# Four PSUM banks for the second product behind attention, and router constants made later

## The chip, the cores and the metric

The program runs on one core of one Trainium2 chip. The metric is the time of one execution on the device in microseconds (us). The kernel before has a median of 832.97 us over three runs (830.79, 832.97 and 835.6).

## The reference

Attention (512 local and 32 global keys, 4 batches, 8 heads) gives x of 2176 tokens by 512. A feed-forward layer follows, and then eight experts, to which a router gives the tokens.

```
def _moe_ref(x, w_in, w_out, alpha):
    h = x @ w_in                                        # 2176 x 512 by 512 x 2048
    g = np.maximum(h, 0.0) + alpha * np.minimum(h, 0.0)
    return (g @ w_out).astype(np.float32)               # 2176 x 2048 by 2048 x 512

def _moe2_ref(x, w_gate, w1, w2):
    logits = x @ w_gate
    order = np.argsort(-logits.flatten())
    # in this order each token goes to its best expert that has room (2176 // 8 = 272 tokens)
    for e in range(E):
        mask = assigned == e
        h = np.maximum(x[mask] @ w1[e], 0.0)
        out[mask] = h @ w2[e]
```

## The kernel before

The tokens are cut into eight blocks (c = 0 to 7) of 272. The hidden width of 2048 is cut into two halves (hf = 0, 1) of eight tiles of 128 (f = 0 to 7). Products are in three terms: each operand is split into a high half (a copy on ACT, L72) and a low half (a subtraction, L73, on DVE or on POOL), and TensorE adds high by high, low by high and high by low.

All eight blocks first pass through half 0 in `gemm`. The first product (`gemm1`, L196) makes tile f in 12 matmuls into a PSUM bank; ACT makes `neg` (L201), DVE makes `g` (L202), ACT its high half `ghi` and POOL its low half `glo`. The second product (L230) makes four outputs d = 0 to 3, each of 8 tiles by three terms, 24 matmuls: 96 for a block. ACT copies each output out of its bank into `xd` (L236; two buffers), and SP sends it to `xpart` in DRAM (L237). The second product has one pool of two banks, `pY`: outputs 2 and 3 reuse the banks of 0 and 1. The order is: output 0 and output 1 over tiles 0 to 5, output 0 and output 1 over tiles 6 and 7, then output 2 and output 3 over all eight tiles.

While attention runs (blocks 0 to 2 and a part of block 3), attention and `gemm` take turns. Behind attention a pool `pO` of two banks is opened, and the first product takes its banks from `pH` (two banks) and `pO` in turn, which is what the list `odd` says (it is empty under attention). In this stretch the weights of half 1 are decoded beside the products (lines 83 to 92; every seventh step, so many steps being six matmuls each), and TensorE turns decoded parts of `w_out` (L132, L140, L146) between the steps. Then half 1's first product runs for all blocks in `gemm1b`, with the logits; then half 1's second product with the router beside it; then the experts.

The order of TensorE's instructions is the order of the program, written out by hand. ACT, DVE, POOL and SP work through queues whose order a planner makes beforehand from a simulated timeline: what is ready goes first, and of what is ready, what stands first in the program. Each engine works its queue in order. `tc.issue_after(x)` puts an edge from each instruction traced in its block to x, but only for the instructions on the engine of x.

Behind the last block of half 0 stand the router's constants (L691 to L779): index tables made by iotas on POOL, small conversions on DVE, and eight memsets on POOL (`ohs`, `gs`, `vas`, `sbs`, twice each). After them stands `splitx(0, 1)`, which makes the high and low halves of block 0 for half 1: `xh` on ACT, `xl` on DVE.

Of the kernel before, what the change touches and what calls it, by code (L numbers as in the profile page):

```python
# [9 lines left out]
F32 = mybir.dt.float32  # L10
# [15 lines left out]
def tile_attention_moe_moe(ctx: ExitStack, tc: tile.TileContext, qkw, vw,  # L26
# [10 lines left out]
    KD = DM // 128  # L37
# [5 lines left out]
    KH = KF // 2  # L43
    CH = CAP
    NCH = NTOK // CH
    CPB = ST // CH
# [24 lines left out]
    def split(hi, lo, src, lo_eng=None):  # L71
        a = A.copy(hi, src)  # L72
        return a, (lo_eng or V).tensor_tensor(lo, src, hi.bitcast(F32), op=OP.subtract)  # L73
# [84 lines left out]
    pH = ctx.enter_context(tc.tile_pool(name="pH", bufs=2, space=PSUM))  # L158
    g1 = ExitStack()
    pY = g1.enter_context(tc.tile_pool(name="pY", bufs=2, space=PSUM))  # L160

    X, XB, alt = {}, {}, {}

    def loadx(c, hf):
        cs = slice(c * CH, (c + 1) * CH)
        X[c, hf] = [None, None]
        if hf:
            t = gx.tile([128, 2, KD, CH], F32, name="xb", bufs=2)
            for i, src in enumerate((xs, xpart)):
                nc.sync.dma_start(out=t[:, i], in_=src[:, :, cs].rearrange("k p t -> p k t"))  # L170
                X[c, hf][i] = t[:, i]

    def splitx(c, hf):
        if hf and c in alt:
            xh, xl = alt[c]
        else:
            xh = gx.tile([128, KD, CH], F32R, name="xh")
            xl = gx.tile([128, KD, CH], F32R, name="xl")
        split(xh, xl, X[c, hf][0] if hf else XB[c // CPB][:, :, (c % CPB) * CH:(c % CPB + 1) * CH])
        X[c, hf] += [xh, xl]  # L180

    post = []
    epi = [None]
    ybank = [pY, "y"]
    odd = []

    def gemm1(c, hf, f, g):
        _, _, xh, xl = X[c, hf]
        wi = WI[hf]
        pool, tag = odd[0] if odd and f % 2 else (pH, "h1")  # L190
        ps = pool.tile([128, CH], F32, name="h1", tag=tag)
        fs = slice(f * 128, (f + 1) * 128)
        i = 0
        for k in range(KD):
            for w, x in ((0, xh), (0, xl), (1, xh)):
                T.matmul(ps, wi[:, w, k, fs], x[:, k], start=i == 0, stop=i == 3 * KD - 1)  # L196
                i += 1
            if k % 2 == 1 and k < KD - 1:
                yield 0.7
        neg = gh_.tile([128, CH], F32, name="neg")  # L200
        A.activation(out=neg, in_=ps, func=AF.Relu, scale=-1.0)  # L201
        epi[0] = V.scalar_tensor_tensor(g, neg, al1[:, hf * KH + f:hf * KH + f + 1], ps, op0=OP.mult, op1=OP.add)  # L202

    def gemm(c, hf, nxt):
        if len(X[c, hf]) < 3:
            splitx(c, hf)
        if nxt is not None:
            loadx(*nxt)
        gh = gt_.tile([128, KH, CH], F32R, name="ghi", tag="ghi")
        gl = gt_.tile([128, KH, CH], F32R, name="glo", tag="glo")  # L210
        wo = WO[hf]
        for f in range(KH):
            g = gh_.tile([128, CH], F32, name="g")
            yield from gemm1(c, hf, f, g)
            split(gh[:, f], gl[:, f], g, lo_eng=P)
            if post:
                post.pop(0)()
            yield 0.7
        if (c + 1, hf) in X:
            splitx(c + 1, hf)  # L220
        ys = {}
        for d, fs in [(0, range(KH - 2)), (1, range(KH - 2)), (0, range(KH - 2, KH)), (1, range(KH - 2, KH))] + [
                (d, range(KH)) for d in range(2, KD)]:
            if d not in ys:
                ys[d] = ybank[0].tile([128, CH], F32, name="y", tag=ybank[1])
            ps = ys[d]
            ds_ = slice(d * 128, (d + 1) * 128)
            for f in fs:
                for i, (w, x) in enumerate(((0, gh), (0, gl), (1, gh))):
                    T.matmul(ps, wo[:, w, f, ds_], x[:, f], start=f == 0 and i == 0, stop=f == KH - 1 and i == 2)  # L230
                if f % 2 == 1 and f < KH - 1:
                    yield 0.7
            if fs[-1] < KH - 1:
                continue
            xd = gx.tile([128, CH], F32, name="xd", bufs=2)
            A.copy(xd, ps)  # L236
            nc.sync.dma_start(out=xpart[d, :, c * CH:(c + 1) * CH], in_=xd)  # L237
            yield 0.7
        X[c, hf] = None
# [25 lines left out]
    LR = 512  # L265
# [22 lines left out]
    def gemm1b(c, nxt):  # L288
        pt = X[c, 1][1]
        for f in range(KH):  # L290
            yield from gemm1(c, 1, f, gbt(c, f))
            if post and f % 2:
                post.pop(0)()
            if f == 0 and nxt is not None:
                loadx(*nxt)
            if f == 4 and nxt is not None:
                splitx(*nxt)
            yield 0.7
        lp = []
        post.append(lambda: lp.append(logits(c, pt)))  # L300
        post.append(lambda: lput(c, lp[0]))

    with ExitStack() as at:
# [308 lines left out]
        c = 0  # L612
        g = None
        going = True
        while going:
            want = c if g is None else c + 1
            if want < NCH and (want, 0) not in X and done[0] >= (want // CPB + 1) * UPB - 1 and (
                    g is None or len(X[c, 0]) == 4):
                loadx(want, 0)
            if g is None and (c, 0) in X:  # L620
                g = gemm(c, 0, None)
            if spent["a"] <= spent["g"] * ratio or g is None:
                x = next(att, None)
                if x is None:
                    going = False
                else:
                    spent["a"] += x
            else:
                x = next(g, None)
                if x is None:  # L630
                    g = None
                    c += 1
                else:
                    spent["g"] += x
                    if parts:
                        f, i = parts.pop(0)
                        with tc.issue_after(at_norm[UPB // 2 - 1, STEPS - 1].ins):
                            f(dc, 0, i)
                    else:
                        share[0] = False  # L640
# [4 lines left out]
    with tc.tile_pool(name="dc2", bufs=1, side="right") as dc, tc.tile_pool(name="pW", bufs=2, space=PSUM) as pW, \  # L645
            tc.tile_pool(name="pO", bufs=2, space=PSUM) as pO:
        odd.append((pO, "h3"))
        more = []
        parts = [(win_part, i) for i in range(2 * KD)] + [(wout_part, i) for i in range(KH)]
        n = 0  # L650
        while c < NCH:
            if g is None:
                if (c, 0) not in X:
                    loadx(c, 0)
                g = gemm(c, 0, (c + 1, 0) if c + 1 < NCH else None)
            while next(g, None) is not None:
                n += 1
                if n % 7 == 0 and parts:
                    f, i = parts.pop(0)
                    with tc.issue_after(epi[0].ins):  # L660
                        more += [(n + 11 + 3 * j, x) for j, x in enumerate(f(dc, 1, i) or [])]
                if more and n >= more[0][0]:
                    more.pop(0)[1]()
            g = None
            c += 1
        assert not parts
        for _, f in more:
            f()
    NDEF = 8
    DEF = list(range(NCH - NDEF, NCH))  # L670
    with ExitStack() as mo:
        rc_ = mo.enter_context(tc.tile_pool(name="rc_", bufs=1, side="right"))
        g2 = ExitStack()
        gx2 = g2.enter_context(tc.tile_pool(name="gx2", bufs=1, side="right"))
        g1.close()
        p4 = mo.enter_context(tc.tile_pool(name="q4", bufs=2, space=PSUM))
# [1 line left out]
        px = mo.enter_context(tc.tile_pool(name="qx", bufs=1, space=PSUM))  # L678
        ph = mo.enter_context(tc.tile_pool(name="qh", bufs=1, space=PSUM))
        pm = mo.enter_context(tc.tile_pool(name="qm", bufs=2, space=PSUM))  # L680
        ybank[:] = [p4, "h4"]

        SH = [26, 20, 15, 10, 5, 0]
        TH = [64, 64, 32, 32, 32, 32]
# [2 lines left out]
        MAGIC = 0x4B000000  # L687
        MF = float(1 << 23)
        MR = 1.5 * MF
        ip = rc_.tile([128, 1], I32, name="ip")  # L690
        P.iota(ip, [[0, 1]], base=0, channel_multiplier=1)  # L691
        ipf = rc_.tile([128, 1], F32, name="ipf")
# [78 lines left out]
        for i in range(2):  # L771
# [5 lines left out]
            P.memset(vas[i], 0.0)  # L777
            sbs.append(rc_.tile([128, NP, 32], BF, name=f"sbs{i}"))
            P.memset(sbs[i], 0.0)  # L779
        Lrow = gx2.tile([128, LR], F32, name="Lrow")  # L780
        loadx(0, 1)
        splitx(0, 1)
        GT = 30
        gbs = [wa.tile([128, GT, CH], F32, name="gb", tag=t) for t in ("wa1", "wa0")]
        gbs.append(gx2.tile([128, NDEF * KH - 2 * GT, CH], F32, name="gb2"))
# [58 lines left out]
        def listing(k, pos):  # L844
# [3 lines left out]
            V.tensor_scalar(ra_h, pos, 1.0 / LB, -0.5 - 0.5 / LB, op0=OP.mult, op1=OP.add)  # L848
            V.tensor_scalar(ra, ra_h, MR, -MR, op0=OP.add, op1=OP.add)
            rb = rt.tile([128, NT], F32, name="rb")  # L850
# [508 lines left out]
        for k in range(E):  # L1359
# [3 lines left out]
            for x in slot(k):  # L1363
# [7 lines left out]
                if gath is not None:  # L1371
                    left -= x
                    if left <= 0:
                        y = next(gath, 0)
# [89 lines left out]
```

## Time and profile before

| | |
|---|---|
| median of three runs | 832.97 us |
| the profiled execution | 830.71 us, of which the span of its instructions 828.9 us |
| mean granted TensorE clock | 0.991 |
| TensorE busy in matmuls | 793.3 us, 96% of the span |
| DVE, ACT, POOL busy | 472.7, 394.4, 350.6 us |
| second products of blocks 3 to 7 | start at 228.12, 252.98, 283.14, 312.32 and 340.43 us |
| first matmul of half 1 | 356.85 us |

Times are counted from the start of the span. A busy TensorE is not TensorE at its peak, since matmuls overlap; what tells of lost time is the distance from the start of one product to the start of the next, against that of a product without a wait. Idle time of an engine counts only where the end waits for it.

### The profile page before, as it was taken

To read this page: it belongs to the slowest core of one execution; us is meant where nothing else is said; L and a number is where in the kernel's file an instruction comes from. 1 tells how busy PE (TensorE), PEld (TensorE's weight loads), DVE (VectorE), ACT (ScalarE), POOL (GpSimd) and SP (SyncE) were. 2 spreads that over 40 slices of the span, in tenths; PEclk is the share of its full clock that TensorE was granted. 3 is DMA by queue.
4 is the path that set the end of the run, shared out by engine and by line. 5 is a ranking of instruction groups with operands and counts; after the bars stand their busy time and mean duration, and the time that the engine had idled before them with its cause. 6 is when DMAs were issued, how large, how long until landed. Compare 5 with 4: busy or idle time off the path is not lost.

```text
span 828.9 us, 20981 instructions
## 1 busy us (share of the span) xinstructions
PE 793.3 (96%) x8328; PEld 736.8 (89%) x8328; DVE 472.7 (57%) x1681; ACT 394.4 (48%) x982; POOL 350.6 (42%) x305
## 2 busy tenths in 40 slices
PE   7989999999998999899999999999999999999995
PEld 5767778988998999799999999999899999999995
DVE  6899955364267664623334357777677777651120
ACT  6786646564454554323333334342455655454421
POOL 1134322020145443400000465663689989688501
PEclk9999999999998999999999999999999999999998
DMA  9975642631245242003131215424366676466201
GB/s 352 393 286 196 206 151 80 229 130 49 65 151 170 65 129 81 9 21 108 55 108 55 82 53 183 153 58 161 86 203 213 209 219 179 146 193 211 92 27 38
DMA packets 49083, 115.99 MB, mean 140 GB/s; under 512 B 4456, under 2 KB 22312, under 8 KB 46937
## 3 DMA queue, kind: packets, MB, share of 16 engines
q1 hardware_dynamic: 46089, 105.74, 39.4%
q0 software_dynamic: 2896, 8.92, 3.0%
q8 instruction: 65, 1.06, 0.5%
q14 instruction: 33, 0.27, 0.1%
HBM read 96.80 MB, written 17.83 MB: 138 GB/s over the span
## 4 chain that ended last, share of the span: by engine, by line
PE 44%; issue 6%; POOL 3%; DMA 2%; DVE 2%; ACT 1%; POOLq 0%; SPq 0%; ACTq 0%
PE h L196 12%; PE h L1218 10%; PE h L1105 7%; PE h L1087 6%; POOL m L73 2%; DMA raw<-in_moe_w_dram 2%; PE lp L273 1%; PE h L1295 1%; PE pc L923 1%; PE y L230 1%; PE yt L251 1%; PE xt L1067 1%; POOL out_dram L1139 1%; POOL xg L1035 1%; DVE gs L889 0%
## 5 line engine op out<-in xcount | busy, mean ns | idle before, releaser
L196 PE MATMUL h<-xh,win 128*128 128x272 f32 x768 | 161.6, 298 | 2.8 <-ACT win L72 1.2
L73 POOL TENSOR_TENSOR m<-raw,m 128x1024 fp32r<-128x1024 f32 x64 | 152.2, 2398 | 17.3 <-ACT m L72 12.8
L196 PEld LDWEIGHTS h<-xh,win 128*128 128x128 f32 x768 | 125.0, 189 | 11.9 <-issue 4.2
L230 PE MATMUL y<-ghi,wout 128*128 128x272 f32 x512 | 112.6, 303 | 6.7 <-ACT xd L236 2.9
L73 POOL TENSOR_TENSOR glo<-g,ghi 128x272 fp32r<-128x272 f32 x64 | 54.5, 856 | 137.1 <-ACT ghi L72 127.0
L196 PE MATMUL h<-xl,win 128*128 128x272 f32 x384 | 111.3, 290 | 0.0
L73 POOL TENSOR_TENSOR gr<-gb,gr 128x272 fp32r<-128x272 f32 x64 | 47.9, 784 | 148.0 <-ACT gr L72 147.5
L1105 PE MATMUL h<-hh,m 128*128 128x272 f32 x512 | 103.8, 294 | 0.0
L1087 PE MATMUL h<-xsh,m 128*128 128x272 f32 x512 | 103.1, 293 | 0.7 <-DVE hl L1093 0.7
L230 PEld LDWEIGHTS y<-ghi,wout 128*128 128x128 f32 x512 | 85.3, 193 | 13.0 <-issue 3.6
L1218 PE MATMUL h<-gr,wout 128*128 128x272 f32 x672 | 95.1, 294 | 0.0
L201 ACT ACTIVATE neg<-h 128x272 f32<-128x272 f32 x128 | 50.4, 395 | 81.1 <-PE h L196 79.0
L1218 PEld LDWEIGHTS h<-gr,wout 128*128 128x128 f32 x672 | 87.0, 189 | 0.4 <-ACT gr L72 0.4
L72 ACT CAST m<-raw 128x1024 fp32r<-128x1024 f32 x64 | 65.9, 1049 | 41.6 <-DMA raw<-in_moe_w_dram 40.9
L1105 PEld LDWEIGHTS h<-hh,m 128*128 128x128 f32 x512 | 81.5, 188 | 1.5 <-issue 1.5
L1087 PEld LDWEIGHTS h<-xsh,m 128*128 128x128 f32 x512 | 81.6, 188 | 0.9 <-DVE hl L1093 0.9
L230 PE MATMUL y<-glo,wout 128*128 128x272 f32 x256 | 75.5, 296 | 2.8 <-POOL glo L73 2.8
L1105 PE MATMUL h<-hl,m 128*128 128x272 f32 x256 | 75.3, 294 | 0.0
L1087 PE MATMUL h<-xsl,m 128*128 128x272 f32 x256 | 73.9, 292 | 0.0
L196 PEld LDWEIGHTS h<-xl,win 128*128 128x128 f32 x384 | 72.9, 190 | 0.4 <-DVE xl L73 0.4
L202 DVE SCALAR_TENSOR_TENSOR g<-neg,al,h 128x272 f32<-128x272 f32 x64 | 35.7, 560 | 59.1 <-ACT neg L201 51.0
L389 ACT ACTIVATE pr<-sc,mx 128x128 f32<-128x128 f32 x128 | 49.9, 392 | 31.2 <-DVE mx L387 31.2
(262 smaller groups left out, 1538.7 us busy)
## 6 DMA issues: line engine op xcount, KB each, us to landing
raw<-in_moe_w_dram SPq DMA_DIRECT2D x64, 512.0 KB, 3.9
vv<-in_v_dram SPq DMA_DIRECT2D x16, 1024.0 KB, 5.9
qk<-in_qk_dram SPq DMA_DIRECT2D x14, 720.0 KB, 8.4
raw<-in_moe_w_in_dram SPq DMA_DIRECT2D x16, 512.0 KB, 7.6
raw<-in_moe_w_out_dram SPq DMA_DIRECT2D x16, 512.0 KB, 5.9
xs<-xb SPq DMA_DIRECT2D x16, 272.0 KB, 6.9
xpart<-xd SPq DMA_DIRECT2D x32, 136.0 KB, 2.2
xb<-xs SPq DMA_DIRECT2D x8, 544.0 KB
```

Of the source, the lines that this page charges most:

```text
L72: a = A.copy(hi, src)
L73: return a, (lo_eng or V).tensor_tensor(lo, src, hi.bitcast(F32), op=OP.subtract)
L196: T.matmul(ps, wi[:, w, k, fs], x[:, k], start=i == 0, stop=i == 3 * KD - 1)
L201: A.activation(out=neg, in_=ps, func=AF.Relu, scale=-1.0)
L202: epi[0] = V.scalar_tensor_tensor(g, neg, al1[:, hf * KH + f:hf * KH + f + 1], ps, op0=OP.mult, op1=OP.add)
L230: T.matmul(ps, wo[:, w, f, ds_], x[:, f], start=f == 0 and i == 0, stop=f == KH - 1 and i == 2)
L251: T.transpose(t[:, k * 128:(k + 1) * 128], xo[:, k, a:b], ident)
L273: T.matmul(lp[r:r + 32], w, x, start=n < 4, stop=n >= LT - 4)
L389: A.activation(out=d["pr", j][:, ii], in_=sc, func=AF.Exp, bias=d["mx", j][:, ii:ii + 1], scale=-1.0, accum_out=d["sm", j][:, ii:ii + 1])
L1087: T.matmul(ps, d["w1"][:, w, kk, f * 128:(f + 1) * 128], x[:, kk], start=kk == 0 and i == 0, stop=kk == KD - 1 and i == 2)
L1105: T.matmul(ps, d["w2"][:, w, f, ms], x[:, f], start=i == 0, stop=i == 3 * K3 - 1)
L1218: T.matmul(ps[j], wo[:, w, f, ds_], x, start=f == 0 and a == 0, stop=f == KH - 1 and a == 2)
```

## The change

In `gemm` the second product looks at `odd`. Where `odd` is not empty (behind attention), outputs 0 and 1 take the banks of `pY`, output 2 one of `pH`, output 3 one of `pO`, and the order is: all four outputs over tiles 0 to 5, then all four over tiles 6 and 7. Under attention order and banks stay. The list `ybank` goes; the later stage that set it does not call `gemm`.

The load and the split of block 0 for half 1 move ahead of the router's constants, and the constants are traced in a block that puts each of them that runs on DVE behind the subtraction that makes `xl`. Those on POOL get no edge.

```diff
-        split(xh, xl, X[c, hf][0] if hf else XB[c // CPB][...])
+        st = split(xh, xl, X[c, hf][0] if hf else XB[c // CPB][...])
         X[c, hf] += [xh, xl]
+        return st[1]
...
-        for d, fs in [(0, range(KH - 2)), (1, range(KH - 2)), (0, range(KH - 2, KH)), (1, range(KH - 2, KH))] + [
-                (d, range(KH)) for d in range(2, KD)]:
+        most, rest = range(KH - 2), range(KH - 2, KH)
+        if odd:
+            parts2 = [(d, x) for x in (most, rest) for d in range(KD)]
+        else:
+            parts2 = [(d, x) for x in (most, rest) for d in range(2)] + [(d, range(KH)) for d in range(2, KD)]
+        for d, fs in parts2:
             if d not in ys:
-                ys[d] = ybank[0].tile([128, CH], F32, name="y", tag=ybank[1])
+                pool, tag = (pY, "y") if d < 2 or not odd else (pH, "h1") if d == 2 else odd[0]
+                ys[d] = pool.tile([128, CH], F32, name="y", tag=tag)
...
+        Lrow = gx2.tile([128, LR], F32, name="Lrow")
+        loadx(0, 1)
+        quiet = ExitStack()
+        quiet.enter_context(tc.issue_after(splitx(0, 1).ins))
         ip = rc_.tile([128, 1], I32, name="ip")
         P.iota(ip, [[0, 1]], base=0, channel_multiplier=1)
...
-        Lrow = gx2.tile([128, LR], F32, name="Lrow")
-        loadx(0, 1)
-        splitx(0, 1)
+        quiet.close()
```

## Rows read from the trace of the kernel before

**Rows 1.** The page: busy time of TensorE, its share of the span, its matmuls.
```profile
PE   793.3 (96%) x8328; PEld 736.8 (89%) x8328; DVE 472.7 (57%) x1681; ACT 394.4 (48%) x982; POOL 350.6 (42%) x305
```

**Rows 2.** Busy time by stretch (us, number): half 1's first product; the experts up to 765.
```profile
357.00:467.00 110.00, 110.00 (x950) 103.09 (x949) 40.20 (x77) 35.38 (x81) 0.00 (x0) 1.00 0.21 63
...
632.00:765.00 133.00, 131.37 (x1165) 127.88 (x1164) 83.94 (x355) 69.77 (x120) 115.66 (x62) 1.00 0.64 195
```

**Rows 3.** By product: length; PE, PEld, DVE, ACT, POOL busy (number); clock; DMA share; GB/s.
```profile
228.12:240.87 12.75, 12.35 (x98) 12.12 (x97) 8.66 (x15) 6.34 (x14) 4.89 (x5) 1.00 0.45 163
240.87:252.98 12.11, 12.11 (x99) 12.11 (x98) 7.55 (x14) 7.57 (x19) 6.50 (x7) 1.00 0.36 117
252.98:271.03 18.05, 15.21 (x98) 14.77 (x97) 11.40 (x14) 7.01 (x14) 7.62 (x7) 0.81 0.55 178
...
283.14:297.38 14.24, 13.43 (x107) 13.03 (x105) 10.40 (x15) 7.10 (x15) 7.13 (x7) 1.00 0.49 140
297.38:312.32 14.94, 14.94 (x122) 13.95 (x121) 8.83 (x15) 9.28 (x22) 7.61 (x8) 1.00 0.27 81
312.32:326.29 13.97, 13.29 (x108) 13.07 (x106) 7.35 (x12) 7.06 (x15) 5.39 (x5) 1.00 0.35 111
326.29:340.43 14.14, 14.14 (x115) 13.15 (x113) 6.06 (x23) 6.24 (x15) 6.55 (x15) 1.00 0.04 12
340.43:356.85 16.42, 13.14 (x99) 12.29 (x98) 7.76 (x25) 3.60 (x8) 4.98 (x8) 1.00 0.08 27
```

**Rows 4.** TensorE's waits from 200 to 360 us: total us, times, longest.
```profile
PE y L230 <- ACT xd L236: 2.9, 3, 1.4
PE y L230 <- POOL glo L73: 2.8, 4, 1.4
PE y L230 <- ACT ghi L72: 2.4, 2, 1.6
```

**Rows 5.** Timeline of TensorE: start, duration, instruction, idle before and its releaser.
```profile
259.63 0.40 PE L230 MATMUL y<-glo,wout 128*128 128x272 f32 x1 [1.45 <-POOL glo L73]
...
262.30 0.59 PE L230 MATMUL y<-ghi,wout 128*128 128x272 f32 x1 [1.39 <-ACT xd L236]
...
344.10 0.39 PE L230 MATMUL y<-ghi,wout 128*128 128x272 f32 x1 [1.62 <-ACT ghi L72]
```

**Rows 6.** Two microseconds of block 4's second product, columns as in Rows 3.
```profile
264.00:266.00 2.00, 2.00 (x11) 2.00 (x10) 0.59 (x1) 0.65 (x2) 0.68 (x1) 0.50 1.02 361
```

**Rows 7.** Timeline of DVE around the router's constants.
```profile
338.07 5.09 DVE L745 TENSOR_SCALAR jt<-j 128x64 int32<-128x64 int32 x1
...
338.80 4.80 DVE L202 SCALAR_TENSOR_TENSOR g<-neg,al,h 128x272 f32<-128x272 f32 x1
...
343.85 0.17 DVE L748 TENSOR_SCALAR thr<-jt 128x64 int32<-128x64 int32 x1
...
344.68 0.48 DVE L202 SCALAR_TENSOR_TENSOR g<-neg,al,h 128x272 f32<-128x272 f32 x1
...
346.20 1.45 DVE L73 TENSOR_TENSOR xl<-xb,xh 128x1088 fp32r<-128x1088 f32 x1
...
347.87 0.49 DVE L202 SCALAR_TENSOR_TENSOR g<-neg,al,h 128x272 f32<-128x272 f32 x1
```

**Rows 8.** Timeline of POOL around the same constants.
```profile
338.54 1.06 POOL L775 MEMSET gs<- 128x1152 bf16 x1
...
342.48 0.63 POOL L779 MEMSET sbs<- 128x640 bf16 x1
344.13 0.76 POOL L73 TENSOR_TENSOR glo<-g,ghi 128x272 fp32r<-128x272 f32 x1 [1.02 <-ACT ghi L72]
```

**Rows 9.** Tile xd from 220 to 360 us: its copies, and their DMAs' time to landing.
```profile
L236 ACT COPY xd<-y x20: 368/387/390, 234.3 to 357.1; 128x272 f32<-128x272 f32 x20
...
DMA to landing us min/median/max: 1.7/2.2/5.1
```

**Rows 10.** The page's DMA issues: size and median us to landing.
```profile
raw<-in_moe_w_in_dram SPq DMA_DIRECT2D x16, 512.0 KB, 7.6
```

More of the change, by code (lines that the diff above doesn't have):

```diff
@@ L178, in splitx @@
             xl = gx.tile([128, KD, CH], F32R, name="xl")
-        split(xh, xl, X[c, hf][0] if hf else XB[c // CPB][:, :, (c % CPB) * CH:(c % CPB + 1) * CH])
+        st = split(xh, xl, X[c, hf][0] if hf else XB[c // CPB][:, :, (c % CPB) * CH:(c % CPB + 1) * CH])
         X[c, hf] += [xh, xl]
+        return st[1]
     post = []
     epi = [None]
-    ybank = [pY, "y"]
     odd = []
@@ L680, in tile_attention_moe_moe @@
         pm = mo.enter_context(tc.tile_pool(name="qm", bufs=2, space=PSUM))
-        ybank[:] = [p4, "h4"]
         SH = [26, 20, 15, 10, 5, 0]
```

## The prediction, made before the change was run

> **What bounds the kernel now.** I read the page first: TensorE is busy 96% of the span [rows 1], so time is to be had only where TensorE waits or runs slowly. Busy time by stretch comes next. From the first matmul of half 1 TensorE does not pause for 110 us, and in the experts it works 131.37 of 133 us [rows 2]: what comes before these stretches moves them, and a microsecond saved ahead of them should arrive at the end nearly whole, since the router and the experts' loads follow on the logits made there. The change touches the second products of blocks 3 to 7, so I cut that stretch at the starts of the products.
>
> A product of 96 matmuls with nothing in its way takes 12.11 us (the one from 240.87) [rows 3], 0.126 us a matmul. Some have turned weights between their steps. The first product of block 6 (14.94) holds three L132 groups, one L140 and one L146; that of block 7 (14.14) holds one L132, one L140 and one L146. So two L132 groups cost 0.80. The second products of blocks 5 and 6 hold two each, the others none. What each second product takes beyond that is its loss:
>
> block 3: 12.75 - 12.11 = 0.64
> block 4: 18.05 - 12.11 = 5.94
> block 5: 14.24 - 12.11 - 0.80 = 1.33
> block 6: 13.97 - 12.11 - 0.80 = 1.06
> block 7: 16.42 - 12.11 = 4.31
>
> Together 13.28 us [rows 3]. The waits say why: three for a bank (the copy xd of an earlier output), 2.9 us; four for a low half glo, 2.8; two for a high half ghi, 2.4 [rows 4]. The rest of the loss is restart, and in block 4 the clock. There two waits stand close together, 1.45 us for the low half of tile 7 and 1.39 us for a bank [rows 5], and behind them the granted clock is 0.50, the lower of the two levels (1.2 of 2.4 GHz), 11 matmuls in 2 us instead of 16 [rows 6]; 0.81 over the product. Of block 4's 5.94 the waits are 2.84, so some 3.1 is clock and restart.
>
> **The change part by part.** The number of matmuls and of steps stays: 16 steps of six matmuls, so the turned weights fall on the same steps. What moves is when a tile is needed and a bank is free.
>
> *Four banks.* Outputs 2 and 3 no longer wait for the copies of 0 and 1. Their banks in pH and pO last held first-product tiles 4 and 5 (one further allocation in each pool lies between), emptied long before. The three waits for a bank go: all of blocks 5 and 6, 1.33 + 1.06 = 2.39, and the second wait of block 4.
>
> *Tiles 6 and 7 later.* They were needed after 36 matmuls, 4.5 us after the start; now after 72, 9.1 us. Block 4's low half of tile 7 came 6.65 us after the start (259.63 - 252.98), so that wait goes too. With both gone nothing I see lowers the clock: the whole 5.94. Bounds: 0, if the waits return elsewhere, to 5.94. I take 5.94, since both waits have their row and each is removed by order alone. Tile 5 is needed when it was before, after 15 matmuls, so block 3's loss (a wait for glo of tile 5) stays: gain 0, at most 0.64.
>
> *The constants.* In block 7 a TENSOR_SCALAR among the constants lasted 5.09 us, where one of the same shape takes 0.17, and g of tile 5 behind it 4.80; the one ended at 343.16, as POOL's run of memsets did (338.54 to 343.11), the other its own half microsecond later [rows 7, 8]. Tiles 6 and 7 got their g only at 344.68 and 347.87, among and behind further constants [rows 7]. That made all four waits of block 7, the longest 1.62 [rows 5]. With DVE's constants behind xl, which cannot come before tile 7 has left the buffer of xh, DVE has nothing but g's to do here, and tile 5's g should end near 339.3. But POOL's memsets get no edge. They wait for the end of the weights' work, as before, and I expect them again ahead of tile 5's glo: 343.11 + 0.76 = 343.87 [rows 8]. TensorE wants it after 16 matmuls, 340.43 + 2.02 = 342.45. So 1.42 of wait remains, 1.5 with restart; tiles 6 and 7 are now due near 351 and safe. Gain 4.31 - 1.5 = 2.8. Bounds: 4.31, if the planner puts glo among the memsets; 0, if DVE is held all the same.
>
> The Trainium skill, SBUF — State Buffer, section "Who interferes with whom", says that a GpSimd instruction and a DVE instruction in a two-port mode exclude each other whole, while a DVE instruction with at most one SBUF input outside these modes does not meet GpSimd at all. By that rule g (neg from SBUF, h from PSUM) was held only as the one queued behind the TENSOR_SCALAR, and goes free once the constants are gone. A row that bears on it: the g at 344.68 took 0.48 beside a POOL instruction that ran from 344.13 to 344.89. If g were itself held by memsets, TensorE would resume near 344.9 as before and the gain of this part would be 1.8 instead of 2.8; the sum would be 1.0 smaller.
>
> The constants themselves are short and fall behind xl, into the tail of block 7 and the start of half 1, where DVE is busy 40.2 of 110 us [rows 2]; the router needs them 100 us later. Nothing.
>
> *What it adds.* All four outputs now end within the last 24 matmuls, 0.76 apart, where copies were 3 us apart, and xd has two buffers. Count from E, the end of the product. Output 0 ends at E - 2.27; its copy takes 0.39 and its DMA lands after 2.2 (median; 1.7 to 5.1) [rows 9]. Output 2 then copies from E + 0.3 to E + 0.7, output 3 until E + 1.5. Its pH bank is wanted by the next block's third tile at E + 3.03, the pO bank by the fourth at E + 4.54. Queued behind the waiting copies on ACT is neg of the next tile 0, due at E + 1.5; its bank is wanted again only at E + 6. So at the median nothing; at the longest landing output 2's bank is free at E + 3.6, 0.6 late. Bounds: 0 to four times 0.6 (behind block 7 the queues are empty). On SP a store that waits holds the weight loads queued behind it for as long. I take 0.9 for one late landing with restart.
>
> *Sum.* 5.94 + 2.39 + 2.8 - 0.9 = 10.2 us. The profiled execution took 830.71, so 820.5. That execution lies 2.3 below the median of the runs shown; the changed kernel's runs will scatter likewise, and I go half of that way: 821.5.
>
> **The rivals.**
>
> *DVE becomes the bound in block 4.* DVE is busy 11.40 us there [rows 3], with decoding. In 12.11 us that is 94%, in a queue that works in order: a g behind a decoding step comes late, tile 5 is late in output 0, and the loss of block 4 is paid again, clock included. Against it: over the five blocks DVE is far from full, and the decoded parts are turned only several us after they are ready. All of 5.94 lost: 826.4.
>
> *The gain does not arrive.* The front gets shorter, but the experts, where POOL is busy 115.66 of 133 us [rows 2], are paced by weights and not by TensorE. Against it: their order hangs on the router, which starts earlier by as much. About 830.
>
> *Slower: the two xd buffers behind full DMA queues.* The stores share the queue with 512 KB weight loads that land after 7.6 us (median) [rows 10]. It decides from the landing at which output 2's copy ends after E + 3.03: 2.27 + 3.03 - 2 x 0.39 = 4.5 us. At 7.6 each of four boundaries (after blocks 3 to 6) loses 3.1, 12.4 in all, and with one more fall of the clock (3.1, as in block 4) 15.5. Without the 0.9 the sum stands at 819.6; with this it is 835.1. For it: SP issues in order. Against: the same stores landed in at most 5.1 us in this stretch [rows 9].
>
> **How the numbers follow.** The forecast 0.65 (own range 816 to 826), DVE as the bound 0.17, no gain 0.10, slower 0.08. A measurement of this kernel tells about 0.5% (4.2 us, 828.8 from the median) from no change. Half of the DVE case comes out near that bound and is counted as same: faster 0.65 + 0.09 = 0.74, same 0.08 + 0.10 = 0.18, slower 0.08. The low end is all 13.28 saved with some luck in the planner's order (816); the high end takes in the no-gain case (831) and leaves the slower one out.
>
> **What would show it.** Right: the distances between the products' starts of blocks 4 to 6 fall to 12.1 plus turned weights, no lower clock there, one wait for glo in block 7 of about 1.4 us, no TENSOR_SCALAR of 5 us, and half 1 starts near 346.6 (356.85 - 10.2). Wrong: waits of the first products' third and fourth tiles for xd; a granted clock of 0.50 anywhere from 228 to 357; tile 5 late in block 4; or half 1 earlier by ten and the end not.

## The result, and the profile after

The changed kernel takes 826.18 us (median of five runs, 824.31 to 826.66); the kernel before, timed beside it, 831.52. The ratio is 0.9913 with a 95% interval of 0.9892 to 0.9935: about 7 us faster by the ratio, 5.3 by the medians. Forecast were 821.5 and a saving of 10.2. The direction and most steps hold; the saving is a half (by the medians) to seven tenths (by the ratio) of the forecast, and the time lies just above the forecast's own range (816 to 826). A second set of eleven runs gave 826.81, ratio 0.9931 (0.9910 to 0.9952).

The profiled execution took 826.46 us, its span 824.7. Its line of TensorE on the page answers to [rows 1]:

```profile
PE 791.3 (96%) x8328; PEld 735.5 (89%) x8328; DVE 470.4 (57%) x1681; ACT 393.2 (48%) x982; POOL 351.2 (43%) x305
```

Below are the same products as in [rows 3], cut at their starts, columns as there. The new code stands five lines lower from the second product on (L235 for L230, L241 for L236).

```profile
230.38:242.92 12.54, 12.34 (x98) 12.11 (x97) 8.46 (x15) 5.31 (x11) 4.91 (x5) 1.00 0.41 149
242.92:255.24 12.32, 12.32 (x98) 12.14 (x97) 6.97 (x13) 7.88 (x21) 5.87 (x7) 1.00 0.38 110
255.24:267.31 12.07, 12.07 (x99) 12.07 (x97) 11.83 (x15) 5.39 (x10) 7.00 (x6) 1.00 0.57 190
267.31:283.04 15.73, 13.87 (x98) 13.65 (x97) 8.89 (x15) 8.63 (x22) 6.99 (x8) 0.89 0.34 117
283.04:295.97 12.93, 12.93 (x107) 12.93 (x105) 9.55 (x14) 6.51 (x14) 6.95 (x6) 1.00 0.38 124
...
310.90:323.92 13.02, 13.02 (x107) 13.02 (x106) 7.52 (x12) 6.67 (x14) 5.44 (x5) 1.00 0.32 99
...
338.06:351.89 13.83, 12.34 (x98) 12.12 (x97) 6.31 (x34) 2.87 (x6) 5.12 (x8) 1.00 0.04 12
```

Read the first number of each row. The second products of blocks 4, 5 and 6 (12.07, 12.93, 13.02) now hold no more than their matmuls and turned weights. That of block 7 went from 16.42 to 13.83. But a product that had nothing in its way before, the first of block 5 from 267.31, now takes 15.73 instead of 12.11, at a mean clock of 0.89. In the kernel before it was, columns as in [rows 3]:

```profile
271.03:283.14 12.11, 12.11 (x99) 12.11 (x98) 8.68 (x14) 6.40 (x16) 5.50 (x6) 1.00 0.19 56
```

TensorE's waits in the stretch, answering to [rows 4], name why:

```profile
PE h L196 <- ACT xd L241: 1.9, 1, 1.9
PE y L235 <- POOL glo L73: 1.7, 2, 1.5
```

The wait for a copy xd has moved: no longer the second product's matmuls wait for it (L230), but the next block's first product (L196). From the start of block 3's second product to half 1 the kernel before takes 128.73 us, the changed one 121.51 (230.38 to 351.89): 7.22 saved. That stretch is what the change touches, and it is what I compare below. The whole spans differ by only 4.2, for two reasons outside it. Block 3's second product started 2.26 us later in this execution; over thirteen profiles of ten programs, in which TensorE's order is the same up to there, this start lay between 228.12 and 234.07, and the kernel before was profiled at its earliest. The rest, from half 1 to the end, scattered between 471.26 and 472.82, and in these two profiles took 0.76 longer after the change.

### The profile page after: what moved, and what is told of

Same layout as the page of the kernel before. It is cut to its first block, busy times and chain, and to the rows that moved or that the text cites. A ratio compares the mean times of both kernels' runs of the same rounds, so it can differ in the third digit from the quotient of the medians.

```text
span 824.7 us, 20982 instructions
## 1 busy us (share of the span) xinstructions
PE 791.3 (96%) x8328; PEld 735.5 (89%) x8328; DVE 470.4 (57%) x1681; ACT 393.2 (48%) x982; POOL 351.2 (43%) x305
## 4 chain that ended last, share of the span: by engine, by line
PE 60%; DVE 12%; issue 9%; DMA 8%; POOL 7%; ACT 3%; POOLq 0%; SPq 0%; ACTq 0%; DVEq 0%
PE h L196 19%; PE h L1224 10%; PE y L235 8%; POOL m L73 4%; PE h L1093 4%; PE h L1111 4%; DMA raw<-in_moe_w_dram 4%; PE o L423 2%; DVE mag L90 2%; DVE pr L406 2%; DMA xpart<-xd 2%; PE s L386 2%; PE lp L278 1%; PE go L472 1%; DVE mag L92 1%
## 5 line engine op out<-in xcount | busy, mean ns | idle before, releaser
L196 PE MATMUL h<-xh,win 128*128 128x272 f32 x768 | 163.6, 300 | 4.7 <-ACT xd L241 1.9
L196 PEld LDWEIGHTS h<-xh,win 128*128 128x128 f32 x768 | 126.3, 191 | 14.3 <-issue 4.2
L196 PE MATMUL h<-xl,win 128*128 128x272 f32 x384 | 111.9, 292 | 0.0
L235 PE MATMUL y<-ghi,wout 128*128 128x272 f32 x512 | 108.8, 298 | 1.4 <-ACT wout L72 1.4
L235 PEld LDWEIGHTS y<-ghi,wout 128*128 128x128 f32 x512 | 83.0, 188 | 6.6 <-issue 3.6
L235 PE MATMUL y<-glo,wout 128*128 128x272 f32 x256 | 74.0, 290 | 1.7 <-POOL glo L73 1.7
L196 PEld LDWEIGHTS h<-xl,win 128*128 128x128 f32 x384 | 73.8, 192 | 0.0
L202 DVE SCALAR_TENSOR_TENSOR gb<-neg,al,h 128x272 f32<-128x272 f32 x64 | 31.2, 496 | 58.9 <-ACT neg L201 58.9
```

## The experiments

Times of different sets are not compared closely, for the front alone scatters by 6 us; each ratio is to the kernel before in the same set.

**Banks and order alone.** The constants go back to where they were.

```diff
-        Lrow = gx2.tile([128, LR], F32, name="Lrow")
-        loadx(0, 1)
-        quiet = ExitStack()
-        quiet.enter_context(tc.issue_after(splitx(0, 1).ins))
...
-        quiet.close()
+        Lrow = gx2.tile([128, LR], F32, name="Lrow")
+        loadx(0, 1)
+        splitx(0, 1)
```

> The four banks and the new order alone; the constants stand and run as before the change. My theory: DVE's constants are held by POOL's memsets again (a TENSOR_SCALAR of about 5 us), so g and glo of tile 5 of block 7 come late; the second product of block 7 takes about 14.6 us (12.11 plus 2.5), against 13.83 with both parts; all other products of blocks 3 to 7 as in the changed kernel. Time about 1 us above the changed kernel's, some 6 below the kernel before. Rival (the constants did all or nothing in block 7): 13.8, as with both parts, or 16.4, as before.

Measured: 828.28 us, ratio 0.9941 (0.9919 to 0.9963); stretch 122.46. Products of blocks 5 (first) and 7 (second), columns as in [rows 3]:

```profile
269.35:285.19 15.84, 13.87 (x99) 13.65 (x97) 8.87 (x15) 8.71 (x22) 7.07 (x8) 0.89 0.37 119
340.20:354.88 14.68, 12.60 (x99) 12.18 (x97) 7.75 (x25) 3.21 (x7) 4.99 (x8) 1.00 0.03 12
```

Block 7's second product takes 14.68, as my theory had it, and DVE's timeline shows the long TENSOR_SCALAR and the g behind it again, as in [rows 7]:

```profile
337.84 5.10 DVE L749 TENSOR_SCALAR jt<-j 128x64 int32<-128x64 int32 x1
...
338.57 4.80 DVE L202 SCALAR_TENSOR_TENSOR g<-neg,al,h 128x272 f32<-128x272 f32 x1
```

The new loss in block 5 is there without the constants' move: it belongs to the banks and the order.

**The constants alone.** Banks and order as before.

```diff
-        if odd:
+        if False:
...
-                pool, tag = (pY, "y") if d < 2 or not odd else (pH, "h1") if d == 2 else odd[0]
+                pool, tag = pY, "y"
```

> The constants' move alone; banks and order as before the change. My theory: no TENSOR_SCALAR of 5 us, tile 5's glo behind the memsets, a wait of about 1.4 us: the second product of block 7 takes 13.6 to 13.9 instead of 16.42; blocks 3 to 6 as before (block 4 18.05, with the lower clock). Time about 2.7 us below the kernel before. Rival (g itself is held by memsets, not the TENSOR_SCALAR ahead of it): 14.6, about 1.8 us below.

Measured: 831.1 us, ratio 0.9973 (0.9948 to 0.9999); stretch 123.81. Second products of blocks 4 and 7:

```profile
258.38:273.85 15.47, 12.63 (x98) 12.19 (x97) 11.42 (x14) 7.02 (x14) 7.66 (x7) 1.00 0.63 200
343.30:357.41 14.11, 12.61 (x98) 12.18 (x97) 6.30 (x34) 3.26 (x7) 5.12 (x8) 1.00 0.09 31
```

Block 7 takes 14.11, between the two figures and nearer to mine (13.6 to 13.9): one wait of 1.50 us for tile 5's low half is left, and no g is held: the g at 342.74 took 0.50 us beside the memsets. What I had not expected is block 4. Its two waits are those of before, 1.45 and 1.39 us:

```profile
265.03 0.40 PE L235 MATMUL y<-glo,wout 128*128 128x272 f32 x1 [1.45 <-POOL glo L73]
267.70 0.39 PE L235 MATMUL y<-ghi,wout 128*128 128x272 f32 x1 [1.39 <-ACT xd L241]
```

Yet the clock stayed at 1.00, and the product took 15.47 instead of 18.05. So about half of what this kernel's stretch is shorter by (2.58 of 128.73 - 123.81 = 4.92) is a fall of the clock that did not come; block 7 gave 2.31.

**The kernel before, a second look.** Unchanged code.

> The kernel before, a second profile. My theory: the start of block 3's second product (228.12 in the first profile, 230.4 to 234.1 in the others, with the same order of instructions up to there) scatters by itself by some us, and so does the fall of the clock in block 4: the two waits there (1.45 and 1.39 us) are the same, and block 4's second product takes 18 us with the lower clock and 15.5 without. Rival (the change itself delays the front): 228 again, and 18 again.

Measured: 829.8 us in one run; block 3's second product started at 229.00, the stretch took 127.24. Block 4's second product:

```profile
253.69:270.39 16.70, 13.87 (x99) 13.44 (x97) 11.38 (x14) 7.01 (x14) 7.62 (x7) 0.90 0.60 193
```

With waits of 1.42 and 1.41 us it takes 16.70, between the 18.05 of the first profile and the 15.47 of the constants alone: the lower clock came, for a shorter time. The rival (228 and 18 again) is out, and changed kernels start there as early as 229.1. Of the 5.94 us that I had counted as block 4's loss, up to 2.6 hang on when the clock falls and returns.

**Two more xd buffers.** Outputs 2 and 3 get their own, from a new pool `xq`.

```diff
-            xd = gx.tile([128, CH], F32, name="xd", bufs=2)
+            xd = (xq[0] if odd and d > 1 else gx).tile([128, CH], F32, name="xd", bufs=2)
```

> The changed kernel with two more xd buffers behind attention (outputs 2 and 3 have their own two). My theory: the wait of block 5's third tile (1.86 us, and the lower clock behind it) is the price of two buffers, each copy waiting for the landing of the store two before it. With four, the copies of outputs 2 and 3 follow at once; the first product of block 5 takes 12.1 to 12.9 us instead of 15.73, no lower clock; time about 3 us below the changed kernel's. Rival (ACT's queue: the copies stand behind decoding steps that wait for DVE and POOL, and it is these that make them late): still a wait of 1 us or more there, 14 us or more, less than 1.5 us gained.

Measured: 826.78 us, ratio 0.9902 (0.9864 to 0.9939); stretch 119.49, 2.0 shorter than the changed kernel's. The 3 us that I expected in the time are not shown: the changed kernel's own ratio is 0.9913. Both products of block 5:

```profile
270.93:283.40 12.47, 12.36 (x99) 12.13 (x97) 7.83 (x13) 6.94 (x19) 6.07 (x6) 1.00 0.46 139
283.40:297.66 14.26, 13.18 (x107) 12.97 (x105) 10.41 (x16) 8.07 (x17) 7.89 (x7) 1.00 0.40 111
```

The first product is at 12.47 with no lower clock, as my theory had it. But 1.3 of the 3.3 us saved come back in the second product, 14.26 instead of 12.93:

```profile
286.65 0.39 PE L236 MATMUL y<-glo,wout 128*128 128x272 f32 x1 [1.08 <-POOL glo L73]
```

With the first product on time, the low half of tile 5 is late. DVE is busy for 10.41 us there, and a g stands behind a decoding step on it (L90, from 281.71 for 1.14 us; the g at 282.78); POOL then splits a part of w_out just ahead of the low half:

```profile
284.59 1.28 POOL L73 TENSOR_TENSOR wout<-mag,wout 128x512 fp32r<-128x512 f32 x1
285.83 1.50 POOL L73 TENSOR_TENSOR glo<-g,ghi 128x272 fp32r<-128x272 f32 x2
```

This is the rival that I had placed in block 4 (decoding as the bound); it sits in block 5. In the changed kernel the stall ahead of it and the lower clock behind the stall had hidden it; the next experiment shows that the stall alone does not.

**POOL's constants behind the last low half.** An edge for POOL as well.

```diff
+            lastlo[0] = split(gh[:, f], gl[:, f], g, lo_eng=P)[1]
...
         quiet.enter_context(tc.issue_after(splitx(0, 1).ins))
+        quiet.enter_context(tc.issue_after(lastlo[0].ins))
```

> The changed kernel, with the constants that run on POOL put behind the last low half of block 7 as well. My theory: tile 5's glo no longer stands behind the memsets; the wait of 1.49 us goes, the second product of block 7 takes 12.1 to 12.3 us instead of 13.83; the memsets run beside the rest of that product, hidden; time about 1.6 us below the changed kernel's. Rival (the constants, all late now, hold DVE or the start of half 1): the product is short but half 1's first products wait, and no time is gained.

Measured: 823.59 us, ratio 0.9887 (0.9855 to 0.9919); stretch 119.95, 1.56 shorter than the changed kernel's, as expected. Both products of block 5 and block 7's second:

```profile
267.50:281.86 14.36, 12.36 (x98) 12.14 (x97) 7.93 (x14) 7.15 (x19) 6.05 (x6) 1.00 0.40 130
281.86:296.22 14.36, 13.27 (x107) 13.03 (x106) 10.51 (x16) 7.77 (x16) 7.89 (x7) 1.00 0.34 110
338.31:350.38 12.07, 12.07 (x98) 12.07 (x97) 6.62 (x34) 2.77 (x6) 8.03 (x16) 1.00 0.04 14
```

Block 7 has nothing left in its way, 12.07: the remaining wait was the memsets ahead of glo, as forecast. In block 5 the wait for xd was 2.00 us, longer than the 1.86 of the changed kernel, and the clock stayed at 1.00 here:

```profile
272.69 0.39 PE L197 MATMUL h<-xh,win 128*128 128x272 f32 x1 [2.00 <-ACT xd L242]
```

But the second product then waited 1.09 us for the low half of tile 5, as with four xd buffers, and took 14.36 instead of 12.93. Together block 5's two products take 28.72 us here and 28.66 in the changed kernel, where the clock fell: what the lower clock cost in the first product came back in the second.

**Memsets moved, DVE's constants not.** Banks and order new, DVE's constants as before the change, the eight memsets alone behind the last low half.

```diff
+        late_ms = ExitStack()
+        late_ms.enter_context(tc.issue_after(lastlo[0].ins))
         for i in range(2):
             ohs.append(rc_.tile([128, NT + 1, E], BF, name=f"ohs{i}"))
             P.memset(ohs[i], 0.0)
...
+        late_ms.close()
```

> The four banks with DVE's constants where they were before the change (not behind xl), and only POOL's eight memsets put behind the last low half. My theory: it was the memsets that held DVE's TENSOR_SCALAR for 5 us; without them beside it, it takes under 1 us, g of tile 5 comes in time, and block 7's second product takes 12.1 to 12.4 us, against 14.68 with the memsets in front: the move of DVE's constants was not needed. Rival (DVE's many small constants hold the g's by themselves): 13 us or more.

Measured, one run: 823.62 us; stretch 120.23. Block 7's second product, and the TENSOR_SCALAR and the g of tile 5 in DVE's timeline:

```profile
337.26:349.33 12.07, 12.07 (x98) 12.07 (x97) 3.38 (x14) 2.80 (x6) 7.27 (x11) 1.00 0.04 14
```

```profile
335.50 0.15 DVE L750 TENSOR_SCALAR jt<-j 128x64 int32<-128x64 int32 x1
...
335.79 0.48 DVE L203 SCALAR_TENSOR_TENSOR g<-neg,al,h 128x272 f32<-128x272 f32 x1
```

The instruction of 5.10 us takes 0.15, the g 0.48, with all small constants still ahead of the g's. It was the memsets; moving them alone does the whole of what the constants' part can do (12.07), more than moving DVE's constants (13.83).

**Outputs spaced apart.** Two xd buffers, but output 3 over all tiles last.

```diff
-            parts2 = [(d, x) for x in (most, rest) for d in range(KD)]
+            parts2 = [(d, x) for x in (most, rest) for d in range(3)] + [(3, range(KH))]
```

> The changed kernel with its four banks and two xd buffers, but outputs 0, 1 and 2 over tiles 0 to 5, then over tiles 6 and 7, and output 3 over all eight last: the first three outputs end 36, 30 and 24 matmuls before the end instead of 18, 12 and 6. My theory: the bunching of the four copies is the price, so the wait for xd in block 5's first product (1.86 us) goes: 12.1 to 12.5 us instead of 15.73. Then block 5's second product is early and waits about 1 us for the low half of tile 5, as with four xd buffers. From the start of block 3's second product to half 1: 119 to 120 us, against 121.5. Rival (the copies wait for decoding steps ahead of them in ACT's queue, wherever they stand): a wait for xd of 1 us or more stays.

Measured: 825.97 us, ratio 0.9944 (0.9918 to 0.9969); stretch 122.33. Here my theory fell: block 5's first product still waits for xd.

```profile
272.06 0.39 PE L196 MATMUL h<-xh,win 128*128 128x272 f32 x1 [2.05 <-ACT xd L241]
```

The same place in ACT's timeline shows the reason:

```profile
265.67 0.68 ACT L83 ACTIVATE mag<-raw 128x512 f32<-128x512 f32 x1 [1.40 <-POOL win L73]
266.26 0.37 ACT L241 COPY xd<-y 128x272 f32<-128x272 f32 x1
266.95 0.62 ACT L72 CAST win<-mag 128x512 fp32r<-128x512 f32 x1 [0.32 <-DVE mag L92]
267.47 0.38 ACT L241 COPY xd<-y 128x272 f32<-128x272 f32 x1
269.37 0.66 ACT L83 ACTIVATE mag<-raw 128x512 f32<-128x512 f32 x1 [1.52 <-DMA raw<-in_moe_w_out_dram]
271.62 0.78 ACT L241 COPY xd<-y 128x272 f32<-128x272 f32 x2 [1.59 <-DMA xpart<-xd]
```

Output 0 is ready two microseconds sooner, but its copy stands behind a decoding step that waits for POOL, and comes at 266.26; its store is issued at 267.38, on SP behind a weight load that waits for its buffer, and the copy of output 2 runs only at 271.62, when that store has landed (the longest landing of the four was 4.2 us). SP's queue:

```profile
263.64 3.69 SPq L79 DMA_DIRECT2D raw<-in_moe_w_out_dram  x2
267.38 5.44 SPq L242 DMA_DIRECT2D xpart<-xd  x4
```

Each resource in the chain works in order, and spacing the matmuls moves none of the others. So both the theory (two buffers) and its rival (decoding ahead in ACT's queue) have a share: decoding makes the copies late, and with two buffers the landing comes on top; with four, block 5's first product is still 0.3 to 0.5 us over 12.11 (12.47, 12.63 and 12.45 in three profiles). No run takes the copies out from behind the decoding, so its share is read from the queues and not tested.

**Spaced, with late memsets.** The last edit and POOL's edge together.

> The spaced order with POOL's constants behind the last low half; two xd buffers. My theory: as with four xd buffers and the late memsets, about 117.8 us from the start of block 3's second product to half 1, time 3 to 4 us below the changed kernel's. Rival (spacing leaves a wait in block 4 for tile 7's low half, now due after 57 matmuls instead of 75): block 4's second product 12.5 or more.

Measured: 825.01 us, ratio 0.9922 (0.9891 to 0.9952); stretch 120.46, block 5's first product 15.94, block 7's second 12.08, block 4's second 12.58. The theory's 117.8 is missed by the same wait for xd, 2.05 us; the rival's small wait in block 4 is there as well. Spacing is no help.

**Four xd buffers and late memsets.** The two edits together, run twice; the second time beside the changed kernel on one chip.

> The changed kernel with the two further xd buffers and with POOL's constants behind the last low half. My theory: the two gains add: block 5's first product about 12.5 us, its second 14.3 with the wait for tile 5's low half, block 7's second product 12.1; from the start of block 3's second product to half 1 about 117.7 us against 121.5; time 3 to 4 us below the changed kernel's. Rival (with the front this short the next engine is the bound): other products lengthen, the stretch stays above 119.

> The changed kernel once more, timed on one chip beside the version with four xd buffers and late memsets. My theory: the wait of block 5's third tile for xd is there again (1.8 to 2.1 us), its first product 14.2 to 15.9 us as the clock falls or does not; block 7's second product 13.8; the stretch from block 3's second product to half 1 120 to 121.7 us. Rival (the wait for xd was an accident of one execution): 12.1 to 12.5 in that product.

> The version with four xd buffers and POOL's constants behind the last low half once more, on the same chip as the changed kernel. My theory: 117.8 us in the stretch again, and a median 2 to 4 us below the changed kernel's on the same chip. Rival (what is saved in the stretch is lost again before the end): no difference in the medians.

Measured, first set: 824.7 us, ratio 0.9910 (0.9879 to 0.9940), stretch 117.80. Second set: 821.22 us (818.77 to 823.48), ratio 0.9866 (0.9833 to 0.9899), against 826.81 (824.25 to 828.81) for the changed kernel, whose first product of block 5 waited 1.97 us for xd and took 15.84, so the wait was no accident. The whole stretch in the second set, this version and then the changed kernel:

```profile
229.14:346.77 117.63, 116.22 (x922) 113.57 (x921) 73.50 (x139) 59.82 (x134) 57.42 (x65) 1.00 0.33 106
```

```profile
229.21:351.09 121.88, 117.99 (x922) 115.12 (x921) 73.63 (x140) 59.56 (x133) 56.56 (x65) 0.99 0.32 102
```

TensorE's busy time falls with the stretch because a matmul at the lower clock is busy longer (block 5's first product: 13.87 us of it at a clock of 0.89, 12.36 at 1.00). The gains add, 4.25 us in the stretch; the medians differ by 5.6, more than the 2 to 4 that I expected and than the stretch gives, which is left to the scatter of the front and the rest. In the second set this version beats both kernels. The first set by itself does not show it: its ratio of 0.9910 is no better than the 0.9913 that the changed kernel had in its own first set.

## Why the prediction was half right

Step by step, measured losses against 12.11 and the turned weights, in the changed kernel's first profile:

- *Bank waits of blocks 5 and 6 go* (2.39). Right: 12.93 and 13.02 leave 0.02 and 0.11.
- *Tile 7's wait and the second bank wait of block 4 go, and the clock with them* (5.94). Right in what went: 12.07. But I took one execution's price for the price. With the same two waits block 4 took 18.05, 16.70 and 15.47 us, so its mean gain is nearer 4.6 (the mean of the three is 16.74) than 5.94. No run has the new banks without the new order; which wait goes with which is read from the waits alone.
- *Block 3's wait stays* (0.64). Right: 0.43.
- *The constants* (loss 4.31 down to 1.5). Right, mechanism and size: 1.72, one wait for tile 5's glo behind the memsets, 1.49 us against 1.42. That a g goes free of the memsets once DVE's constants are gone was right too: it took 0.50 us beside them in the changed kernel (at 337.50) and with the constants alone (at 342.74). The Trainium skill, SBUF — State Buffer, section "Who interferes with whom", says that a DVE instruction with at most one SBUF input, outside the two-port modes, does not contend with GpSimd; these two times agree. But the move of DVE's constants was not the only way, nor the best: with the memsets moved alone nothing is left (12.07).
- *What it adds* (0.9 for one late landing). This is the step that failed, by its size: 3.62 (15.73 - 12.11). I counted the copies from the end of each output, E - 2.27 for output 0 of block 4; it was copied 0.76 after E, since ACT's queue held decoding ahead of it. Then the landing of its store came on top, which the copy of output 2 waits for, and the clock fell. Two of the prediction's own signs of being wrong came with it: a wait of a first product's third tile for xd, and a granted clock of 0.50. The rows of ACT, SP and TensorE (two microseconds, columns as in [rows 3]) in the changed kernel:

```profile
267.54 0.62 ACT L72 CAST win<-mag 128x512 fp32r<-128x512 f32 x1 [0.59 <-DVE mag L92]
268.07 0.38 ACT L241 COPY xd<-y 128x272 f32<-128x272 f32 x1
269.56 0.67 ACT L83 ACTIVATE mag<-raw 128x512 f32<-128x512 f32 x1 [1.11 <-POOL win L73]
270.13 0.37 ACT L241 COPY xd<-y 128x272 f32<-128x272 f32 x1
271.91 0.83 ACT L241 COPY xd<-y 128x272 f32<-128x272 f32 x2 [1.41 <-DMA xpart<-xd]
```

```profile
268.48 4.65 SPq L242 DMA_DIRECT2D xpart<-xd  x4
```

```profile
274.00:276.00 2.00, 2.00 (x11) 2.00 (x10) 1.97 (x4) 1.04 (x4) 1.45 (x2) 0.50 0.03 8
```

The bank of output 2 was wanted at E + 3.03 = 270.34 and came free at 272.3. This is the mechanism of the slower rival (two xd buffers), at one boundary of four and not all: the other three cost at most 0.21. I had its condition (landings over 4.5 us) from landings alone; a late copy reaches the same point with a landing of 3.4 (268.48 to 271.9). ACT is busy for only 7 us of block 4's 18 in [rows 3], and I took that for room; but an engine may be idle most of the time and still late, when its queue stands in order behind another's work. The decoding ahead of the copy was itself late: its step at L90 on DVE took 1.74 us beside POOL's split of win, and ended 0.55 after it, where the one before had taken 0.69.

```profile
264.95 1.29 POOL L73 TENSOR_TENSOR win<-mag,win 128x512 fp32r<-128x512 f32 x1 [2.47 <-ACT win L72]
265.05 1.74 DVE L90 SCALAR_TENSOR_TENSOR mag<-raw,mag 128x512 int32<-128x512 int32 x1
```

The sum: forecast to remain 0.64 + 1.5 + 0.9 = 3.0 of 13.28; measured 6.1. The difference of 3 us is the boundary behind block 4 (2.7) and small change. Not all of the 2.7 is the price of two buffers: with four, block 5's two products take 26.73 us against 28.66, so 1.9 come back, and the rest stays as the wait for tile 5's low half (1.08), the rival of decoding one block later than I had placed it. Some 1.6 us of the gap between the forecast 821.5 and 826.18 remain, and no run shows whose they are. They are of the size of the scatter: the execution that the sum was made against had the earliest front of thirteen profiles (228.12, the median being 229.34), for which the forecast had added 1.0. The prediction also counts the times of its rivals (826.4 and 835.1) from 820.5 and its forecast from 821.5, so these two stand 1 us too low beside it.

## What to carry to other kernels

When a stall is taken out by letting work end later, ask of each thing that now ends late not when it could start, but what stands ahead of it in the queue of the engine that does it, and what that waits for. Buffers that were plenty at one copy in 3 us are short at four copies in 3 us. A price that holds a fall of the clock is one draw: take it from more than one execution. And a stall can hide another behind it: add up the products on both sides before one product's length is called the price.

## What the runs showed of the hardware

A DVE TENSOR_SCALAR that had begun beside a subtraction on POOL did not get its turn between POOL's instructions: it ended only when the run of seven memsets queued back to back behind that subtraction was over, 5.09 us after its start [rows 7, 8], and 5.10 in the second profile of the kernel before. Where the memsets were moved, the same instruction had no POOL instruction beside it and took 0.15. Another TENSOR_SCALAR met a single glo there; it took 0.81, until that glo was over, against 0.22 in the kernel before:

```profile
334.50 0.81 POOL L73 TENSOR_TENSOR glo<-g,ghi 128x272 fp32r<-128x272 f32 x1
334.58 0.81 DVE L729 TENSOR_SCALAR fr_b<-fr 128x128 int32<-128x128 int32 x1
```

A g, in contrast, ran through the memsets in the changed kernel:

```profile
337.16 0.66 POOL L785 MEMSET vas<- 128x680 bf16 x1
337.50 0.50 DVE L202 SCALAR_TENSOR_TENSOR g<-neg,al,h 128x272 f32<-128x272 f32 x1 [0.85 <-ACT neg L201]
```

The fall of TensorE's clock behind a wait is not settled by the length of the wait. One wait of 1.86 us had it fall to 0.50, one of 2.00 in the same place did not; it came in six of seven profiles with a wait of 1.86 to 2.06 us there. In that product it cost about 1.5 us (15.84 with a wait of 1.97 against 14.36 with 2.00), but nothing by the end of block 5: its two products together took 28.66 to 28.89 us in the six and 28.72 in the one.
